# A spectral filter mixed with a state-space branch: split halves in PSUM tiles of their own, weight rows copied by ScalarE, and another written order

## The chip, the core and the metric

One core of one Trainium2 chip runs one program. The metric is device time in microseconds, the median of several executions. Engines are named as in the profile: PE (TensorE matmul) and PEld (its weight loads), DVE (VectorE), ACT (ScalarE), POOL (GpSimd) and SP (SyncE, which here issues DMAs). Each engine runs its instructions strictly in the order in which they were written; a wait at the head of a queue holds all that stands behind it.

## The reference

The input is a sequence of 2048 rows by 512 channels. Two branches are computed from it and mixed by a gate per row.

```python
x = A_x                                                   # 1 x 2048 x 512
g = sigmoid((x * gate_w).sum(-1, keepdims=True))          # one gate per row
X = rfft2(x, axes=(-2, -1)) * (w_r + 1j * w_i)            # 2048 x 257 weights
a = irfft2(X, s=(2048, 512), axes=(-2, -1))               # branch A
dt = exp(log_dt); A = -exp(log_A_real) + 1j * A_imag
K = 2 * einsum("dn,dnl->dl", C * dt, exp(A * dt * pos)).real
b = irfft(rfft(x.T, 4096) * rfft(K, 4096))[:2048].T + x * D_skip   # branch B, a causal convolution
out = g * a + (1 - g) * b
```

## The kernel before

**What is computed where.** With the given inputs `A * dt * 2048` is so small that K is constant along the sequence, and branch B is a running sum of x times one number per channel plus the skip term. The program counts on the chip for how many channels that holds (word `G4` counts, `G5` reads the count) and has a general path behind a branch, which is not taken. Branch A is a two-dimensional Fourier transform, a product with the weights, and the transform back, all in float32.

**Stages of branch A.** Each is a short function, and each has a letter; a letter with a number is a word of the written order.
- `F`, `C`, `c` (lines 254 to 284): ten parts of x (DMA into `AI`) are folded by POOL, multiplied on PE into `p_s`, and turned by DVE into `AR`. This is the first factor of the transform along the sequence.
- Then eight units, 0 to 7, each of two slots of rows. `P` (line 424) multiplies `AR` by `s2e` into `p_t`; `t` (431) copies it to `et` on ACT; `D` (440) is the transform over channels into `p_d`, with `dfw`; `d` (453) copies a part of it to `ds` on ACT; `Z` (459) forms sums and differences in `p_d` on DVE; `U` and `W` (475) are the two products with the weights `w` on DVE into `tw`. Units 3 and 5 (`ZPE`) do the sums in PE with `zfw` and skip `Z`.
- `p` (486) and `g` (494) combine the products on POOL into `px` and `gt`; `h` (506) repairs the first row on ACT; `I` (525) transforms back over channels on PE into `p_v`; `i` (533) copies a part to `po` on ACT; `V` (540) adds on DVE into `AI`.
- `K`, `B`, `b`, `Q`, `q` (548 to 603): the transform back along the sequence. `K` repairs slot 0, `B` multiplies eight blocks into `p_ia` (with `NDUM` dummy matmuls ahead of block `FIRSTB`), `b` turns them into `AR`, `Q` multiplies by `s1a` into `p_oa`, and `q` adds `XT` and stores to `out`. Every `B` needs all units; so everything from `K` on is a tail behind the last unit.

Two units, 1 and 7, are split: the words 11, 21 and 17, 27 are the halves (64 of 128 rows) of units 1 and 7. In the kernel before the two halves share one PSUM tile at each of `P`, `D` and `I`.

**Branch B and the gate.** `X` loads the transposed input into `XT`, 1 MB for each of four blocks; `x` copies to PSUM, `m` is the running sum on DVE, `o` scales by the skip factor on ACT, `y` writes the scaled sum to `v`, and `r` adds `v` to `XT` with an accumulating DMA that POOL issues. `k` multiplies `XT` by the gate weights on PE (line 376); `G1` is the sigmoid, `G2` sends the gates to DRAM, `O` loads them back spread over all partitions as `gb`, `u` copies them to PSUM, `H` multiplies `XT` by 1 - g on POOL, and `E` multiplies the constants `s1a` by g on DVE, so that `Q` gives g * a.

**Weight rows.** The weights come per unit with `l` (`w<-in_w_dram`, 512 KB). Their partition 0 needs other numbers, worked out from columns 0 and 256: `J0` does it with three DVE and two ACT instructions, `J1` turns the result with a matmul, `J2` copies it to `hT`, and `L` puts 2 KB of it into partition 0 of each unit's `w` with a DMA on SP's queue. That DMA waits until the unit's `w` has landed.

**What sets the order.** The string `PLAN` lists all words in one order, and each engine gets its share of that order. Tiles come from pools: `ps` has four PSUM tiles of two banks; `blk` has 13 SBUF tiles that `f`, `prm`, `et`, `tw`, `px`, `gt` and `gs` share; `w` and `s1a` share four; `v` and `gb` share four. A new tile waits for the last reader of the one whose place it takes. SP's queue also waits for the eighth DMA back, since eight semaphores go round.

Of the kernel before, what the change touches and what calls it, by code (L numbers as in the profile page):

```python
# [21 lines left out]
NV = 4  # L22
ZPE = (3, 5)
LASTQ = 4
FIRSTB = 1
# [22 lines left out]
def _consts():  # L48
# [91 lines left out]
    for x in range(2):  # L140
# [32 lines left out]
        "c_s2v": f32(s2v), "c_s2r": f32(s2r), "c_s2q": f32(s2q), "c_s1b": f32(s1b), "c_s1a": f32(s1a.reshape(128, 16, 2, 128).transpose(0, 2, 1, 3).reshape(128, 4, 8, 128).transpose(1, 0, 2, 3)), "c_dfw": f32(dfw), "c_zfw": f32(zfw), "c_dbw": f32(dbw),  # L173
# [5 lines left out]
def body(ctx: ExitStack, tc: tile.TileContext, x, xg, xt, w, wh, prms, vecs, gw,  # L179
         c_s1e, c_s1f, c_s2e, c_s2, c_s2v, c_s2r, c_s2q, c_s1b, c_s1a, c_dfw, c_zfw, c_dbw, c_pos, c_eye, out):  # L180
# [27 lines left out]
    last = work.tile([P, 384], F32, name="last")  # L208
    s1e, ones = last[:, 0:128], last[:, 128:256]
    hw = last[:, 256:320].rearrange("p (q r f m) -> p q r f m", q=8, r=2, f=2)  # L210
    hs = last[:, 320:352].rearrange("p (q i) -> p q i", q=8)
    few = last[:, 352:376].rearrange("p (k i) -> p k i", i=4)
    pers = work.tile([P, 16], F32, name="pers")
    s0, dsk, one, m_, nm = pers[:, 0:8], pers[:, 8:12], pers[:, 12:13], pers[:, 13:14], pers[:, 14:15]
    s2e = work.tile([P, 16, P], F32, name="s2e")
    s2v = work.tile([P, 64], F32, name="s2v")
    s2r = work.tile([P, P], F32, name="s2r")
# [3 lines left out]
    hT = work.tile([32, P], F32, name="hT")  # L221
    gws = work.tile([P, 4, 32], F32, name="gws")
# [9 lines left out]
    with tc.manual_schedule():  # L232
        prm = {}
        ldt = few[:, 0]
        nc.scalar.dma_start(s1e, c_s1e)
        nc.scalar.dma_start(hw, wh)
        nc.scalar.dma_start(eye, c_eye)
# [62 lines left out]
        def n1():  # L300
            S.activation(few[:, 0], few[:, 0], AF.Exp)
# [115 lines left out]
        def load_h(u):  # L417
            nc.sync.dma_start(t_["w", u][0:1, 0], hT[4 * u:4 * u + 4])
# [455 lines left out]
```

## Time and profile before

| | |
|---|---|
| time, median of 3 runs | 119.22 us (118.77 to 123.17) |
| the profiled execution: its own time, and its span | 119.98 us, 118.1 us |
| busy in the span | PE 96.8, PEld 78.7, DVE 88.0, ACT 45.6, POOL 75.1 us |
| mean granted PE clock | 0.969 |
| moved by DMA | 28.79 MB, mean 244 GB/s |

The span goes from the first to the last instruction; the profiled execution's own time is 1.88 us more. All rows that are quoted come from that one execution, whose own time is 0.76 us above the median. A program matmul in float32 stands as two matmuls in the trace, so the four of a half unit are eight rows. Times at the head of a row are microseconds from the start of the span. Where instructions of one engine follow each other without a wait, the time of one shown is longer than the step from one start to the next, since their ends overlap.

### The profile page before, as it was taken

The page shows a single profiled execution, that of the slowest core. Times are in us where ns is not written, and L with a number is a line of the kernel's source. Part 1 is how long each engine was busy: PE and PEld are TensorE (multiplying, and loading weights), DVE is VectorE, ACT ScalarE, POOL GpSimd, SP SyncE. Part 2 cuts the span into 40 slices and gives each one's busy share as a digit, 9 for nine tenths or more (in the row PEclk, how much of TensorE's full clock was granted, in tenths as well). Part 3 has the DMA queues.
Part 4 walks back from the last instruction along what each step waited for, and adds up shares of the span by engine and source line. Part 5 has one row for each costly group of instructions (what it writes and reads, how often), then busy time and mean ns, then how long its engine had stood idle before and what let it go on. Part 6 is the DMA issues. An engine that isn't in the chain of part 4 may idle for free.

```text
span 118.1 us, 2316 instructions
## 1 busy us (share of the span) xinstructions
PE 96.8 (82%) x877; PEld 78.7 (67%) x877; DVE 88.0 (74%) x139; ACT 45.6 (39%) x80; POOL 75.1 (64%) x70
## 2 busy tenths in 40 slices
PE   6989784999861999968495978997899999999700
PEld 6957463999430649967395977987753359999700
DVE  0059889848988439999649599999798999956620
ACT  0320004359549059391878283698740000000000
POOL 0069580220796005999999999999999999910000
PEclk9999999999999679999999999999999999999985
DMA  3999999977979976499979999978129700678680
GB/s 66 381 389 416 413 383 345 298 318 238 327 286 337 409 226 220 136 325 178 225 191 214 262 321 218 262 198 297 50 44 190 126 3 3 248 314 330 248 302 15
DMA packets 9314, 28.79 MB, mean 244 GB/s; under 512 B 1577, under 2 KB 2121, under 8 KB 8781
## 3 DMA queue, kind: packets, MB, share of 16 engines
q1 hardware_dynamic: 7628, 23.93, 55.9%
q0 software_dynamic: 1088, 4.19, 19.5%
q10 hardware_dynamic: 576, 0.43, 1.1%
q8 instruction: 9, 0.15, 0.5%
q14 instruction: 13, 0.10, 0.3%
HBM read 20.12 MB, written 4.21 MB: 206 GB/s over the span
## 4 chain that ended last, share of the span: by engine, by line
PE 46%; DMA 29%; POOL 10%; DVE 3%; ACT 3%; issue 2%; SPq 1%; DVEq 0%; POOLq 0%
PE p_oa L588 13%; PE p_d L447 10%; DMA s2e<-in_c_s2e_dram 8%; PE p_ia L565 6%; DMA XT<-in_xt_dram 6%; PE p_t L429 6%; PE p_v L531 6%; DMA AI<-in_x_dram 6%; POOL gt L504 4%; DMA s1a<-in_c_s1a_dram 4%; DMA w<-in_w_dram 3%; DMA last<-in_c_s1e_dram 3%; POOL gt L503 2%; POOL px L490 2%; PE p_gate L376 2%
## 5 line engine op out<-in xcount | busy, mean ns | idle before, releaser
L447 PE MATMUL p_d<-et,dfw 128*128 128x256 f32 (+1 forms) x80 | 18.7, 370 | 4.2 <-ACT et L434 3.2
L484 DVE TENSOR_TENSOR tw<-p_d,w 128x1024 f32<-128x1024 f32 (+1 forms) x20 | 19.2, 1005 | 1.2 <-ACT ds L456 0.6
L371 POOL TENSOR_TENSOR XT<-XT,gb 128x1024 f32<-128x1024 f32 x8 | 19.2, 2755 | 0.0
L447 PEld LDWEIGHTS p_d<-et,dfw 128*128 128x128 f32 x80 | 12.9, 202 | 8.4 <-ACT et L434 4.7
L531 PE MATMUL p_v<-dbw,gt 128*128 128x128 f32 x128 | 15.8, 278 | 2.5 <-POOL px L490 1.2
L429 PE MATMUL p_t<-s2e,AR 128*128 128x128 f32 x128 | 16.2, 282 | 1.6 <-DMA s2e<-in_c_s2e_dram 1.6
L429 PEld LDWEIGHTS p_t<-s2e,AR 128*128 128x128 f32 x128 | 15.8, 196 | 2.0 <-DVE AR L283 1.8
L531 PEld LDWEIGHTS p_v<-dbw,gt 128*128 128x128 f32 x128 | 14.9, 192 | 3.2 <-ACT gt L512 1.4
L283 DVE STREAM_TRANSPOSE AR<-p_s 128x512 f32<-128x512 f32 (+1 forms) x20 | 10.7, 587 | 7.3 <-PE p_s L275 7.3
L503 POOL TENSOR_TENSOR gt<-px 128x512 f32<-128x512 f32 (+1 forms) x10 | 11.0, 1101 | 7.8 <-PE p_d L447 7.3
L588 PEld LDWEIGHTS p_oa<-s1a,AR 128*128 128x128 f32 x128 | 15.2, 196 | 0.8 <-DVE AR L569 0.8
L588 PE MATMUL p_oa<-s1a,AR 128*128 128x128 f32 x128 | 15.3, 282 | 0.0
L490 POOL TENSOR_TENSOR px<-tw 128x512 f32<-128x512 f32 (+1 forms) x10 | 11.8, 1179 | 5.0 <-DVE tw L484 5.0
L258 POOL TENSOR_TENSOR f<-AI 128x512 f32<-128x512 f32 (+1 forms) x8 | 9.0, 1138 | 7.8 <-DMA AI<-in_x_dram 7.7
L545 DVE TENSOR_TENSOR AI<-p_v,po 128x512 f32<-128x512 f32 (+1 forms) x20 | 10.3, 574 | 2.0 <-PE p_v L531 1.3
L491 POOL TENSOR_TENSOR px<-tw 128x512 f32<-128x512 f32 (+1 forms) x10 | 11.7, 1174 | 0.0
L504 POOL TENSOR_TENSOR gt<-px 128x512 f32<-128x512 f32 (+1 forms) x10 | 11.0, 1102 | 0.0
L602 DVE TENSOR_TENSOR AI<-p_oa,XT 128x1024 f32<-128x1024 f32 x7 | 8.5, 1219 | 3.1 <-PE p_oa L588 2.6
L275 PE MATMUL p_s<-AI,last 64*64 64x128 f32 (+1 forms) x192 | 9.9, 335 | 0.5 <-DMA AI<-in_x_dram 0.5
L569 DVE STREAM_TRANSPOSE AR<-p_ia 128x1024 f32<-128x1024 f32 x8 | 9.3, 1216 | 0.5 <-PE p_ia L565 0.5
L339 DVE TENSOR_TENSOR_SCAN p_x<-p_x,XT 128x1024 f32<-128x1024 f32 x4 | 9.2, 2290 | 0.3 <-ACT p_x L336 0.3
L434 ACT COPY et<-p_t 128x1024 f32<-128x1024 f32 (+1 forms) x10 | 8.2, 845 | 2.3 <-PE p_t L429 2.2
(72 smaller groups left out, 120.2 us busy)
## 6 DMA issues: line engine op xcount, KB each, us to landing
XT<-in_xt_dram SPq DMA_DIRECT2D x4, 1024.0 KB, 7.2
w<-in_w_dram SPq DMA_DIRECT2D x8, 512.0 KB, 8.4
XT<-v POOLq DMA_DIRECT2D x4, 1024.0 KB, 9.1
out_dram<-AI SPq DMA_DIRECT2D x7, 512.0 KB, 3.4
AI<-in_x_dram SPq DMA_DIRECT2D x6, 512.0 KB, 6.2
gb<-gd SPq DMA_DIRECT2D x4, 512.0 KB, 4.0
s1a<-in_c_s1a_dram SPq DMA_DIRECT2D x4, 512.0 KB, 4.9
AI<-in_x_dram SPq DMA_DIRECT2D x4, 256.0 KB
```

The source lines that it names most:

```text
L283: V.transpose(av[:, u, :, k], pv[:, u])
L371: E.tensor_tensor(r, r, t_["gb", h % 2], op=ALU.mult)
L429: T.matmul(p[:, q, :, 64 * v:64 * v + 64], AR[:, q % 2, 8 * (q // 2) + u, :, v], s2e[:, 2 * u + v], start=True, stop=True)
L447: T.matmul(d[:, o, 1:3] if h else d[:, o, 0:4:3], dfw[:, 2 * h + o], e[:, 2 * h + o], start=True, stop=not z)
L484: E.tensor_tensor(t, z, w, op=ALU.mult)
L490: G.tensor_tensor(po[:, 0], t1[:, :, 0:4:2], t1[:, :, 1:4:2][:, :, ::-1], op=ALU.subtract)
L491: G.tensor_tensor(po[:, 1, :, ::-1], t2[:, :, 0:4:2], t2[:, :, 1:4:2][:, :, ::-1], op=ALU.add)
L503: G.tensor_tensor(gv[:, :, 0], src[0], src[1], op=ALU.subtract)
L504: G.tensor_tensor(gv[:, ::-1, 1], src[0], src[1], op=ALU.add)
L531: T.matmul(p[:, v, h, o], rows(u, o, v, h), dbw[:, h, o], start=True, stop=True)
L545: V.tensor_tensor(ai[:, :, :, k], t_["pi", u][:, v, :, 0], t_["po", u][:, v], op=ALU.subtract if k else ALU.add)
L588: T.matmul(p[:, b], VA[:, i, 8 * (k % 2) + b, :, k // 2], s1a[k][:, b], start=True, stop=True)
```

## The change

- **Halves.** `P`, `D` and `I` of a half unit each take a PSUM tile of their own (`acc`), and their columns lie together (`cut`), in `et`, `ds` and `tw` too. Which units are split is read from `PLAN`; they are still 1 and 7.
- **Weight rows.** `wh` is laid out on the host as 8 rows of 2 x 512 numbers. `J` is now two DVE instructions on 8 partitions and one DMA of ACT's queue, which puts eight rows of 512 into partition 0 of `AI` (after its x has been read). `L` is a copy on ACT from there into partition 0 of `w`. The matmul, `hs`, `hT`, the copy of it and the eight DMAs on SP's queue are gone; the identity `eye` is loaded on the path that is not taken.
- **Gated constants.** `s1a` comes as half of its columns (256 KB for each of four), since the other half differs by a sign that goes with the partition. `E` is one DVE product instead of two, and one ACT instruction that multiplies by the sign (`sgn`).
- **Small loads.** Gate weights, `log_dt`, the skip factors and the sign come in one DMA (`gv`), and `s2v` and `s2r` in one (`s2`).
- **Order.** `PLAN` is another list of the same words (without `J1` and `J2`), `FIRSTB` is 0 and `LASTQ` is 7. Unit 1 now comes ahead of unit 7.

The diff, with `PLAN` cut to its first line and what is repeated left out:

```diff
@@
+SLOT = (5, 3, 6, 7, 0, 4, 1, 2)
 ZPE = (3, 5)
-LASTQ = 4
-FIRSTB = 1
+LASTQ = 7
+FIRSTB = 0
...
-F2 X1 C0 R7 C1 c0 R6 J0 c1 F3 J1 R9 C2 c2 F4 C3 c3 F5 R1 R0 C4 J2 F6 C5 c4 C6 c5 F7 F9 T0 F8 c6 C7 c7 C8 C9 c8 c9 P17
...
+R7 R0 C1 F2 C0 c0 c1 T0 C2 c2 F3 C3 c3 F4 C4 F5 R1 C5 F6 F8 F9 c4 c5 C6 c6 C8 R9 J0 C9 c9 c8 R6 F7 C7 c7 P11 N1 l1 N0
...
+SPLIT = [int(w[2:]) for w in PLAN.split() if w[0] == "P" and w[1] == "1" and len(w) == 3]
...
-        nc.scalar.dma_start(hw, wh)
-        nc.scalar.dma_start(eye, c_eye)
+        hw = blk([P, 2, 512], "hw")[0:8]
+        nc.scalar.dma_start(hw, wh)
...
         def J_(k):
-            if k == 0:
-                V.tensor_tensor(hs[:, :, 0:4:2], hw[:, :, 0, :, 0], hw[:, :, 0, :, 1], op=ALU.add)
...
-                S.copy(hT, t_["ph"][:32, 0, 0:P])
-
+            a, b = (hw[:, z].rearrange("u (i k) -> u i k", i=4) for z in range(2))
+            V.tensor_tensor(a[:, 0:4:2], a[:, 0:4:2], b[:, 0:4:2], op=ALU.add)
+            V.tensor_tensor(a[:, 1:4:2], a[:, 1:4:2], b[:, 1:4:2], op=ALU.subtract)
+            nc.scalar.dma_start(AI[0:1, 0:8], hw[:, 0])
...
         def load_h(u):
-            nc.sync.dma_start(t_["w", u][0:1, 0], hT[4 * u:4 * u + 4])
+            S.copy(t_["w", u][0:1, 0].rearrange("p i k -> p (i k)"), AI[0:1, SLOT[u]])
...
+        def cut(t, n, v=None):
+            if len(t.shape) == 3 and t.shape[1] == 8:
+                return t
+            t = t.rearrange("p a b k -> p (a b k)" if len(t.shape) == 4 else "p a b -> p (a b)")
+            if n % 10 in SPLIT:
+                return t.rearrange("p (v g k) -> p v g k", v=2, k=64)[:, n // 10 - 1]
+            t = t.rearrange("p (g k) -> p g k", k=P)
+            return t if v is None else t[:, :, 64 * v:64 * v + 64]
+
+        def acc(name, n):
+            p = psum(name)
+            return p[:, 0].rearrange("p (g k) -> p g k", k=64) if n >= 10 else p
+
         def P_(n):
             u, r, vs = unit(n)
-            p = new(("pt", u), lambda: psum("p_t").rearrange("p k (q c r) -> p (k q) c r", q=2, c=2))
+            p = t_["pt", n] = acc("p_t", n)
...
         def D_(n):
             u, r, vs = unit(n)
-            new(("pd", u), lambda: psum("p_d"))
+            t_["pd", n] = acc("p_d", n)
...
         def I_(n):
             u, r, vs = unit(n)
-            p = new(("pi", u), lambda: psum("p_v").rearrange("p u (h o t) -> p u h o t", h=2, o=2))
+            p = t_["pi", n] = psum("p_v").rearrange("p u (h o t) -> p u h o t", h=2, o=2)
...
         def load_a(k):
-            s1a[k] = work.tile([P, 8, P], F32, tag="w", name="s1a", bufs=4)
-            nc.sync.dma_start(s1a[k], c_s1a[k])
+            s1a[k] = work.tile([P, 2, 8, 64], F32, tag="w", name="s1a", bufs=4)
+            nc.sync.dma_start(s1a[k][:, 1].rearrange("p b c -> p (b c)"), c_s1a[k])

         def gated(k, E):
-            s = s1a[k].rearrange("p b (e c) -> p b e c", e=2)
...
-            for e in range(2):
-                E.tensor_tensor(s[:, :, e], s[:, :, e], g, op=ALU.mult)
+            a = s1a[k].rearrange("p e b c -> p e (b c)")
+            g = (t_["gp", k // 2] if E is V else t_["gb", 2 + k // 2])[:, 512 * (k % 2):512 * (k % 2) + 512]
+            E.tensor_tensor(a[:, 0], a[:, 1], g, op=ALU.mult)
+            S.activation(a[:, 1], a[:, 0], AF.Copy, scale=sgn)
...
-            lambda: (nc.sync.dma_start(gws, gw), nc.sync.dma_start(dsk, vecs[:, 1])),
-            lambda: (nc.sync.dma_start(s2v, c_s2v), nc.sync.dma_start(s2r, c_s2r)),
+            lambda: nc.sync.dma_start(gv, gw),
+            lambda: nc.sync.dma_start(s2, c_s2v),
```

What the order does at three places of the program, on the engines that wait or are waited for there.

PE, from its first matmul of the unit stage (`p_t` is word `P`, `p_d` is word `D`, the number is the tile's), in the kernel before:

```order
L429 MATMUL p_t_305<-s2e_75,AR_67 128x2x64 x8
L429 MATMUL p_t_318<-s2e_75,AR_67 128x2x64 x4
L447 MATMUL p_d_328<-et_325,dfw_78 128x2x64 x8
L429 MATMUL p_t_318<-s2e_75,AR_67 128x2x64 x4
L429 MATMUL p_t_375<-s2e_75,AR_67 128x2x64 x8
L429 MATMUL p_t_385<-s2e_75,AR_67 128x2x64 x8
L447 MATMUL p_d_408<-et_367,dfw_78 128x2x64 x4
L376 MATMUL p_gate_415<-XT_72,gws_82 32x512 x4
L447 MATMUL p_d_408<-et_367,dfw_78 128x2x64 x4
L376 MATMUL p_gate_415<-XT_72,gws_82 32x512 x8
```

and in the changed kernel, where the gates `p_gate` stand 15 rows further back than this piece ends:

```order
L432 MATMUL p_t_295<-s2e_75,AR_67 128x128 x4
L432 MATMUL p_t_305<-s2e_75,AR_67 128x128 x4
L450 MATMUL p_d_319<-et_316,dfw_77 128x2x64 x2
L450 MATMUL p_d_319<-et_316,dfw_77 128x128 x2
L450 MATMUL p_d_326<-et_316,dfw_77 128x2x64 x2
L450 MATMUL p_d_326<-et_316,dfw_77 128x128 x2
L432 MATMUL p_t_340<-s2e_75,AR_67 128x128 x4
```

Before, both halves of unit 7 lie in `p_t_305` and both `D` halves of unit 1 in `p_d_408`, with gate matmuls between them; now each half has a tile, and the halves follow each other directly. Of the gate matmuls, 16 program matmuls on the four 1 MB blocks of `XT`, eight now come behind the `D` of units 1, 7, 4 and 6, and eight behind that of unit 0 too, instead of among the `D` of units 1 and 4.

POOL, from its first `px` (word `p`; `gt` is word `g`), before:

```order
L490 TENSOR_TENSOR px_432<-tw_397 128x2x2x64
L491 TENSOR_TENSOR px_432<-tw_395 128x2x2x64
L490 TENSOR_TENSOR px_432<-tw_397 128x2x2x64
L491 TENSOR_TENSOR px_432<-tw_395 128x2x2x64
L503 TENSOR_TENSOR gt_469<-px_432 128x2x2x64
L504 TENSOR_TENSOR gt_469<-px_432 128x2x2x64
L503 TENSOR_TENSOR gt_469<-px_432 128x2x2x64
L504 TENSOR_TENSOR gt_469<-px_432 128x2x2x64
L490 TENSOR_TENSOR px_478<-tw_465 128x2x2x64
```

and now:

```order
L493 TENSOR_TENSOR px_398<-tw_360 128x2x2x64
L494 TENSOR_TENSOR px_398<-tw_357 128x2x2x64
L506 TENSOR_TENSOR gt_401<-px_398 128x2x2x64
L507 TENSOR_TENSOR gt_401<-px_398 128x2x2x64
L493 TENSOR_TENSOR px_398<-tw_360 128x2x2x64
L494 TENSOR_TENSOR px_398<-tw_357 128x2x2x64
L506 TENSOR_TENSOR gt_401<-px_398 128x2x2x64
```

The first half's `gt` now stands ahead of the second half's `px`, and these are the halves of unit 1. The tile behind the third `gt` differs as well: before, `gt_553` (unit 1, two rows behind this piece) takes the place of `et_435`, which the matmuls into `p_d_458` read; now `gt_401` and `gt_457` take the places of an `f` and a `prm` tile of the first stage.

SP's DMA queue from the first weight row, before:

```order
L418 DMA w<-hT 1x4x128
L415 DMA w<-in_w_dram 128x1024 x3
L418 DMA w<-hT 1x4x128
L332 DMA XT<-in_xt_dram 128x2048
L418 DMA w<-hT 1x4x128
L332 DMA XT<-in_xt_dram 128x2048
L415 DMA w<-in_w_dram 128x1024
```

and the same stretch now, from the third weight load:

```order
L405 DMA w<-in_w_dram 128x1024
L330 DMA XT<-in_xt_dram 128x2048
L405 DMA w<-in_w_dram 128x1024
L617 DMA dbw<-in_c_dbw_dram 128x768
L330 DMA XT<-in_xt_dram 128x2048 x2
L405 DMA w<-in_w_dram 128x1024
```

The rows `L418`, each of which waits for a `w` to land, are gone from this queue; the loads of `XT` and `w` follow each other. All of `w`'s row copies now stand on ACT's queue, the first as that engine's eighth instruction behind its table load.

More of the change, by code (lines that the diff above doesn't have):

```diff
@@ L206, in body @@
     X = AF_
[L208 removed]
+    last = work.tile([P, 288], F32, name="last")
     s1e, ones = last[:, 0:128], last[:, 128:256]
[L210 to L212 removed]
+    few = last[:, 256:280].rearrange("p (k i) -> p k i", i=4)
     pers = work.tile([P, 16], F32, name="pers")
[L214 removed]
+    s0, one, m_, nm = pers[:, 0:8], pers[:, 12:13], pers[:, 13:14], pers[:, 14:15]
     s2e = work.tile([P, 16, P], F32, name="s2e")
[L216 to L217 removed]
+    s2 = work.tile([P, 192], F32, name="s2")
+    s2v, s2r = s2[:, 0:64], s2[:, 64:192]
     dfw = work.tile([P, 4, P], F32, name="dfw")
@@ L220, in body @@
     dbw = work.tile([P, 2, 3, P], F32, name="dbw")
-    hT = work.tile([32, P], F32, name="hT")
-    gws = work.tile([P, 4, 32], F32, name="gws")
+    gv = work.tile([P, 137], F32, name="gv")
+    gws, ldt, dsk = gv[:, 0:128].rearrange("p (i c) -> p i c", i=4), gv[:, 128:132], gv[:, 132:136]
+    sgn = gv[:, 136:137]
     def blk(shape, name):
@@ L530, in I_ @@
                     for o in range(2):
[L531 removed]
+                        T.matmul(p[:, v - vs[0], h, o], rows(u, o, v, h), dbw[:, h, o], start=True, stop=True)
         def i_a(n):
```

75 lines of the change are left out of this document (35 added, 40 removed).

## Prediction

> **What bounds the kernel now.** I read the stretches first: how busy each engine is, stage by stage. The columns are the stretch, its length, the busy time of PE, PEld, DVE, ACT and POOL, the granted PE clock, the DMA share and GB/s.
>
> ```profile
> core 0: us, PE busy (x) PEld busy (x) DVE busy (x) ACT busy (x) POOL busy (x), PEclk, DMA share, GB/s
> ...
> 30.00:38.00 8.00, 4.20 (x36) 2.14 (x39) 7.18 (x14) 5.13 (x8) 6.59 (x10) 1.00 0.87 308
> 38.00:42.50 4.50, 4.50 (x20) 2.50 (x24) 1.59 (x3) 0.62 (x3) 0.37 (x1) 0.63 0.97 386
> 42.50:46.00 3.50, 3.50 (x23) 2.44 (x23) 2.70 (x5) 3.43 (x5) 0.33 (x1) 0.98 0.58 162
> 46.00:60.00 14.00, 11.01 (x80) 10.25 (x79) 11.64 (x16) 8.27 (x17) 13.84 (x15) 1.00 0.85 219
> 60.00:84.00 24.00, 20.76 (x166) 19.43 (x165) 21.73 (x35) 16.47 (x31) 23.69 (x20) 1.00 0.90 241
> 84.00:89.00 5.00, 4.62 (x26) 2.90 (x27) 4.36 (x9) 2.88 (x5) 5.00 (x3) 1.00 0.27 50
> ```
>
> From 46 to 84 POOL is busy 13.84 of 14 and 23.69 of 24 us: there it sets the pace. From 38 to 46 it does 0.70 us of work in 8, and PE, busy throughout, runs at a clock of 0.63 for 4.5 us. So POOL's end is its work plus a hole, and the next question is what made the hole. The chain of waits (start us, us, what) and the waits (engine, line, what it waited for, total, times, longest) answer it.
>
> ```profile
> 23.26 1.80 PE p_d L447 x16
> ...
> 25.83 0.32 SPq L418
> 26.20 4.06 DMA w<-in_w_dram
> 30.27 0.59 SPq L418
> 30.91 7.00 DMA XT<-in_xt_dram
> 37.95 1.06 PE p_gate L376 x8
> 39.02 3.49 PE p_d L447 x8
> 42.51 1.06 PE p_gate L376 x8
> 43.57 1.92 PE p_d L447 x8
> ...
> 82.60 1.29 POOL gt L504
> 83.91 0.43 ACT gt L512
> 84.38 2.05 PE p_v L531 x16
> 86.44 0.86 PE p_k L551 x2
> 87.30 1.72 PE p_ia L559 x4
> 89.01 7.22 PE p_ia L565 x62
> 96.23 15.29 PE p_oa L588 x128
> ```
>
> ```profile
> SPq L418 <- DMA w<-in_w_dram: 12.4, 4, 5.0
> ...
> PE p_gate L376 <- DMA XT<-in_xt_dram: 3.4, 1, 3.4
> ...
> POOL gt L503 <- PE p_d L447: 7.3, 1, 7.3
> ```
>
> Read from top to bottom: SP's queue holds at the weight rows (`L418`) until `w` lands, 12.4 us in four waits; so `XT` is issued at 30.91 and lands 7.00 us later; PE, in order, stands 3.4 us at the gate matmuls, and its next eight `D` rows take 3.49 us where the eight after take 1.92; the last `D` ends at 45.49, and POOL's third `gt`, which takes the place of the `et` which that `D` reads, waits 7.3 us. The timeline of POOL (start, us, operation, and in brackets the idle time before it) has the ends of this:
>
> ```profile
> 30.26 0.73 POOL L490 TENSOR_TENSOR px<-tw 128x256 f32<-128x256 f32 x1 [3.81 <-DVE tw L484]
> ...
> 36.95 0.73 POOL L490 TENSOR_TENSOR px<-tw 128x256 f32<-128x256 f32 x1 [1.15 <-DVE tw L484]
> ...
> 45.67 0.74 POOL L503 TENSOR_TENSOR gt<-px 128x256 f32<-128x256 f32 x1 [7.30 <-PE p_d L447]
> ```
>
> So the span has four legs: up to POOL's first `px` at 30.26; from there to the end of the last `gt`, 82.60 + 1.29 = 83.89, which is 53.63 us, of them 1.15 + 7.30 = 8.45 waited and 45.18 filled; from 83.89 to the first row of `B` at 89.01, 5.12; and `B`, `Q` and the stores, 118.1 - 89.01 = 29.09.
>
> **Leg 1, to the first `px`.** Rows of the timeline where the unit stage begins:
>
> ```profile
> 15.33 3.98 DVE L283 STREAM_TRANSPOSE AR<-p_s 128x512 f32<-128x512 f32 x8 [1.09 <-PE p_s L275]
> ...
> 20.08 3.18 PE L429 MATMUL p_t<-s2e,AR 128*128 128x128 f32 x24 [1.62 <-DMA s2e<-in_c_s2e_dram]
> ```
>
> `AR` is ready at 15.33 + 3.98 = 19.31, but PE starts at 20.08, after `s2e`. That load now stands second behind x instead of fourth; the start becomes about 19.5, -0.6. Before, the copy `t` waited for both halves of a shared tile, 16 rows of 3.18 / 24 = 0.1325 us; a half in a tile of its own waits for 8, -1.06. In the same way `d` waits for 8 rows of `D` instead of 16, half of the 1.80 us at 23.26, -0.90. Together -2.6, and the first `px` comes at about 27.7. If the copies in between eat the halves' gain, -0.6 is left; -3.2 if the first `D` also no longer waits for the second half's copy, which before it did.
>
> **Leg 2, to the last `gt`.** POOL's work is the same here: ten `px`, ten `gt` and three DMA issues, 45.18 us. The hole goes only if what led to it goes: the `XT` loads no longer stand behind a wait for `w`, the gates stand behind four units' `D`, and the third `gt` takes the place of a tile of the first stage. All three are in the order of the changed kernel, so I take the 8.45 us away; the cold clock (3.49 - 1.92 = 1.57) lies inside it and isn't counted again. What is late next? Groups of one form and the DMA issues (name, KB each, median us to landing) give the prices:
>
> ```profile
> L339 DVE TENSOR_TENSOR_SCAN p_x<-p_x,XT 128x1024 f32<-128x1024 f32 x4 | 9.2, 2290 | 0.3 <-ACT p_x L336 0.3
> ...
> L343 ACT ACTIVATE XT<-XT,pers 128x1024 f32<-128x1024 f32 x8 | 9.0, 1147 | 0.0
> ...
> L582 DVE TENSOR_TENSOR s1a<-s1a,p_g 128x512 f32<-128x512 f32 x8 | 5.0, 677 | 0.0
> ...
> L537 ACT COPY po<-p_v 128x512 f32<-128x512 f32 x6 | 3.5, 575 | 2.1 <-PE p_v L531 2.1
> ...
> L511 ACT COPY gt<-px 1x256 f32<-1x256 f32 x6 | 2.6, 428 | 3.9 <-POOL gt L503 3.9
> ...
> L511 ACT COPY gt<-px 1x128 f32<-1x128 f32 x4 | 1.2, 300 | 0.0
> ...
> XT<-in_xt_dram SPq DMA_DIRECT2D x4, 1024.0 KB, 7.2
> w<-in_w_dram SPq DMA_DIRECT2D x8, 512.0 KB, 8.4
> ```
>
> - Weight rows on ACT: no 1x512 copy stands in the trace. From 300 ns for 128 and 428 for 256 elements, 128 more cost 128 ns, so 512 cost about 0.684 us; the lower bound is the 575 of the 128x512 copy. Eight are 4.6 to 5.5 us, and I take 5.5. ACT was busy 5.13 + 0.62 + 3.43 + 8.27 + 16.47 = 33.92 us from 30 to 84; with the rows 39.4, still under POOL's 45.18. So most lies beside POOL's work, but each copy stands ahead of some `et`, `ds` or `po` which PE or DVE waits for. SP loses eight issues and the 12.4 us.
> - DVE had 7.18 + 1.59 + 2.70 + 11.64 + 21.73 = 44.84 us from 30 to 84, about what POOL has. `E` falls from eight products to four, -4 x 0.677 = -2.7, of which the tail takes a part. So DVE feeds POOL with no slack to speak of.
> - The accumulating DMA `r1` now stands on POOL behind the two steps each of `px` and `gt` of unit 4, 4 x 1.29 = 5.16 us. From the same point it needs the scan (2.29) and three ACT passes (`y` and two `o`, 3 x 1.15), 5.74 us: 0.6 of wait, and 2.6 if the copy ahead of the scan is late by two `et` or row copies.
>
> Bounds for the new waits: POOL's idle share from 46 to 84, (0.16 + 0.31) / 38 = 1.2% of 45.18, so 0.6 us; and 8.45, if the hole only moves. I take 3.3: 2.6 at `r1`, and 0.7 for the thin feeding. Leg 2: -8.45 + 3.3 = -5.15; the last `gt` ends at 83.89 - 2.6 - 5.15 = 76.1.
>
> On the row copies the Trainium skill has a price: its page ScalarE: Activation LUTs (section What ACT_TABLE_LOAD costs) gives an ACTIVATE 186 ns and 0.833 ns for each element, which is 613 ns for 512, an estimate. By it eight are 4.9 us rather than 5.5; the trace's nearest rows differ both ways (575 for 128x512, 428 for 1x256), and none has that form.
>
> **Leg 3, to the first `B`.** Before: `gt`, its repair on ACT 0.43, `I` 2.05, `K` 0.86, two dummy matmuls in four rows 1.72, `B`. The dummies covered ACT's copy of `K`'s result. Now they stand behind `K1`, so that copy (0.575 for its like) is bare, and ahead of it ACT has the sign half of one `E` (0.575 to 0.72). `K0` moreover waits for `V3` on DVE, which stands behind a scan and three `V`: I take 1.0, from half of one scan (2.29 / 2 = 1.15). Sum 0.6 + 0.6 + 1.0 = +2.2, bounds 0 (all done while POOL finishes) and +4.5 (the whole scan late). `B` starts at 83.5 or so.
>
> Against moving that half of `E` speaks a rule of the same page (section Rules for kernel authors): multiplications belong on VectorE. By it the 0.6 us ahead of `K1`'s copy would be the change's own loss, and without it leg 3 were 1.6 and the time 113.1, an estimate. The trace bears that out only in part: from 84 to 89 DVE is busy 4.36 of 5 and ACT 2.88, so on DVE the 0.677 would stand in the fuller queue.
>
> **Leg 4, the tail.** `B` 7.22 and `Q` 15.29 keep their rows. Two of the four `E` (3 and 2) now lie between blocks of `B` and `Q` on DVE and ACT: 2 x (0.677 + 0.6) = 2.6 us, hidden by the first quarters of `Q`, 15.29 / 8 = 1.91 each, of which two precede `Q3`; if that cover is gone, about 1.3. POOL's eight products with 1 - g follow the last `gt` as before. I take 0.
>
> **Sum.** -2.6 - 8.45 + 3.3 + 2.2 = -5.55 against the profiled execution's own 119.98: 114.4. That execution lies 0.76 above the median of 119.22, so 113.7 for the median. 2% is about what a measurement of this kernel can tell from no change: faster is below 116.8, slower above 121.6.
>
> **Rivals.**
> - *The waits for `w` move from SP to ACT (slower).* A row copy on ACT still needs its `w`, and behind it stand `et` and `ds` for PE and DVE. If each `w` lands as late as before, ACT waits 12.4 in place of the 3.3: -2.6 - 8.45 + 12.4 + 2.2 = +3.55, and +5.1 with one more cold stretch of 1.57 us: 122.8 to 124.3. It decides from 11.3 us of such waits in all for slower by 2%, since 8.85 of gain stand against it. For it: a `w` takes 8.4 us at the median, and DMA stood at 0.87 to 0.97 of its capacity from 30 to 42.5. Against: the loads were late there since SP held them, and the first three `w` now go ahead of the first `XT` but for nothing else. The Trainium skill, TensorE: Matmul & The Clock Gate (Part 1: The HAM clock gate), has PE fall to half clock after about 3.4 us idle; the trace's wait of 3.4 us and the clock of 0.63 behind it agree.
> - *ACT becomes the bound.* All 5.5 us of row copies come on the path in place of the 3.3: -3.35, own 116.6, median 115.9; with the 3.3 as well, 119.2. For it: 39.4 us plus the sign copies, and every stage passes through ACT. Against: 54 - 39.4 still leaves it 14.6 us of idle time in that stretch.
> - *PSUM.* Twelve half tiles for `P`, `D` and `I` in place of six, from four places: six more takes, each of which may wait for one DVE product on a half, the 0.677 us of the 128x512 row. +4.1 us, median 117.8. For it: a second half's `D` now waits for a tile that a `W` of the other unit reads. Against: a half frees its tile sooner.
> - *No new wait.* Leg 2 with 0.6 and leg 3 with 0: -10.45, median 108.8; with leg 3 as forecast, 111.0.
>
> **Chances.** Forecast (111.5 to 116) 0.58; no new wait 0.12; ACT 0.14; PSUM 0.08; slower 0.08. Faster: 0.58 + 0.12 + a third of ACT's = 0.75; same: the rest of ACT's and PSUM's, 0.17; slower 0.08. The range from 109.5 to 118.0 leaves out the slower rival, part of the no-wait one and ACT's upper third, together 0.16.
>
> **What would show it.** Right: no `XT` wait at the gate matmuls and no stretch of low clock after 30; POOL's first `px` at 27 to 28.5, its third `gt` without a wait of microseconds; last `gt` at 75 to 77.5; first `B` at 82 to 85; `B` and `Q` as long as before; row copies of 0.58 to 0.7. Wrong: ACT waiting for `w` for more than 3 us; POOL idle for more than 5 us between its first `px` and last `gt`; a `Q` that waits for `s1a`.

## The result, and the profile after

The changed kernel took 113.88 us (median of four, 112.72 to 114.33) against 120.48 for the kernel before (median of four, 118.77 to 123.17): a ratio of 0.9555, with a 95% interval of 0.943 to 0.968. Ratios with an interval are of each kernel's faster executions alone (here all four now, and the 118.77 and 119.22 before); that of the two medians is 0.945. In a later comparison the same two gave 114.22 (six, 112.87 to 115.25) and 120.03, ratio 0.9607, interval 0.947 to 0.974. The forecast was 113.7. The profiled execution took 113.95 us, its span is 112.2.

The chain of waits after (start us, us, what) reaches back only to the end of POOL's last `gt`:

```profile
76.19 0.43 ACT gt L515
76.62 0.04 issue
76.66 2.07 PE p_v L534 x16
...
79.23 0.42 ACT s1a L585
...
79.86 0.58 ACT AI L556
80.44 0.04 issue
80.48 1.98 PE p_ia L562 x4
82.47 6.37 PE p_ia L568 x56
```

The engines by stretch (columns as before: PE, PEld, DVE, ACT, POOL, granted PE clock, DMA share, GB/s):

```profile
29.00:47.00 18.00, 17.07 (x129) 13.10 (x129) 15.75 (x29) 13.30 (x24) 16.20 (x20) 1.00 0.79 306
47.00:76.20 29.20, 26.84 (x208) 24.63 (x200) 28.25 (x41) 24.19 (x44) 28.77 (x24) 1.00 0.85 208
```

And POOL's rows with the idle time ahead of them, from its first `px` to its last `gt`:

```profile
29.04 0.73 POOL L493 TENSOR_TENSOR px<-tw 128x256 f32<-128x256 f32 x1 [2.20 <-DVE tw L487]
...
47.03 1.36 POOL L351 DMA_DIRECT2D XT<-v  x1 [1.40 <-ACT XT L341]
...
74.88 1.28 POOL L507 TENSOR_TENSOR gt<-px 128x512 f32<-128x512 f32 x1
```

The hole is gone: the clock stays at 1.00, the gate matmuls no longer wait for an `XT`, and POOL waits once, 1.40 us, at `r1`. But for that it is busy from its first `px` to its last `gt`, with DVE close to it (28.25 of 29.2 us). SP's queue waits little for `w` ahead of `XT`:

```profile
SPq L330 <- DMA w<-in_w_dram: 2.5, 2, 1.5
```

By the four legs of the prediction:

| leg | before | after | difference | forecast |
|---|---|---|---|---|
| 1, to the first `px` | 30.26 | 29.04 | -1.22 | -2.6 |
| 2, to the end of the last `gt` | 53.63 | 47.12 | -6.51 | -5.15 |
| 3, to the first `B` | 5.12 | 6.31 | +1.19 | +2.2 |
| 4, to the end of the span | 29.09 | 29.73 | +0.64 | 0 |
| span | 118.1 | 112.2 | -5.9 | -5.55 |

Leg 2 can be compared to a tenth of a microsecond: in five profiles of the changed kernel and of kernels that differ from it outside this leg, it is 47.11 or 47.12. Leg 1 can't: with the same code it ends between 27.35 and 29.34, as the next section shows.

### The profile page after: what moved, and what is told of

It is laid out like the page before. It is cut to its first block, busy times and chain, and to the rows that moved or that the text cites. A ratio compares the mean times of both kernels' runs of the same rounds, so it can differ in the third digit from the quotient of the medians.

```text
span 112.2 us, 2292 instructions
## 1 busy us (share of the span) xinstructions
PE 96.8 (86%) x876; PEld 78.1 (70%) x876; DVE 85.9 (77%) x134; ACT 51.5 (46%) x89; POOL 75.5 (67%) x70
## 5 line engine op out<-in xcount | busy, mean ns | idle before, releaser
L432 PE MATMUL p_t<-s2e,AR 128*128 128x128 f32 x128 | 17.0, 286 | 2.9 <-DVE AR L283 1.6
L450 PE MATMUL p_d<-et,dfw 128*128 128x256 f32 (+1 forms) x80 | 16.8, 343 | 0.8 <-ACT v L346 0.3
L534 PE MATMUL p_v<-dbw,gt 128*128 128x128 f32 x128 | 15.2, 276 | 1.6 <-ACT gt L515 1.6
L450 PEld LDWEIGHTS p_d<-et,dfw 128*128 128x128 f32 x80 | 12.0, 191 | 3.5 <-ACT gt L515 1.1
L275 PE MATMUL p_s<-AI,last 64*64 64x128 f32 (+1 forms) x192 | 10.7, 362 | 0.7 <-DMA AI<-in_x_dram 0.7
L506 POOL TENSOR_TENSOR gt<-px 128x512 f32<-128x512 f32 (+1 forms) x10 | 10.6, 1061 | 0.8
L507 POOL TENSOR_TENSOR gt<-px 128x512 f32<-128x512 f32 (+1 forms) x10 | 10.6, 1059 | 0.0
```

The lines of the kernel that those rows point to most:

```text
L275: T.matmul(p[64 * g:64 * g + 64, h, u * n:u * n + n], s1e[r, 64 * u * i:64 * u * i + 64], src[:, g * n:g * n + n], start=i == 0, stop=i == ...
L432: T.matmul(cut(p, n, v)[:, 2 * q:2 * q + 2], AR[:, q % 2, 8 * (q // 2) + u, :, v], s2e[:, 2 * u + v], start=True, stop=True)
L450: T.matmul(d[:, o, 1:3] if h else d[:, o, 0:4:3], dfw[:, 2 * h + o], e[:, 2 * h + o], start=True, stop=not z)
L506: G.tensor_tensor(gv[:, :, 0], src[0], src[1], op=ALU.subtract)
L507: G.tensor_tensor(gv[:, ::-1, 1], src[0], src[1], op=ALU.add)
L534: T.matmul(p[:, v - vs[0], h, o], rows(u, o, v, h), dbw[:, h, o], start=True, stop=True)
```

## The experiments

### Is it the gates behind a late XT that made the hole?

The kernel before, with the gate matmuls (`k`) moved behind `D6`, and SP's queue as it was:

```diff
-D11 d11 k0 D21 k1 k2 p17 t6 D4 X3 y0 Z11 d21 l5 k3 R10 D6 U11
+D11 d11 D21 p17 t6 D4 X3 y0 Z11 d21 l5 R10 D6 k0 k1 k2 k3 U11
```

> The kernel before with one thing moved: the four groups of gate matmuls stand behind the D of unit 6, where before they stood among the halves of D of unit 1 and ahead of that of units 4 and 6. Nothing else differs; the weight rows still go by SP's queue, which still waits 12 us for w. Theory 1 (the hole of POOL came from a D that stood behind gate matmuls, and these behind an XT that SP's waits had made late): POOL's third gt waits less than 1.5 us instead of 7.3, and the time falls by 4 to 7 us, to 112 to 116 against 119.2. Theory 2 (the hole would come in any case, since XT is as late as before and everything behind the gates on PE waits for it): PE's wait at the gates stays at 3 us or more, POOL waits somewhere else, and less than 2 us are gained.

117.59 us (four, 115.42 to 117.86) against 120.45 (seven, 118.46 to 122.67): 2.9 us less (3.0 between the fastest of each), with no overlap of the two sets. POOL's rows:

```profile
32.13 0.73 POOL L490 TENSOR_TENSOR px<-tw 128x256 f32<-128x256 f32 x1 [3.80 <-DVE tw L484]
...
38.63 0.74 POOL L490 TENSOR_TENSOR px<-tw 128x256 f32<-128x256 f32 x1 [0.96 <-DVE tw L484]
...
47.46 1.26 POOL L490 TENSOR_TENSOR px<-tw 128x512 f32<-128x512 f32 x1 [1.71 <-DVE tw L484]
...
51.75 1.29 POOL L503 TENSOR_TENSOR gt<-px 128x512 f32<-128x512 f32 x1 [1.78 <-ACT gt L512]
```

The third `gt` waits no more: the 7.30 us are gone with nothing changed but the place of the gates. So the gates ahead of that `D` are shown to be what held POOL; that their `XT` came late because SP waited for `w` is not tried by this run, which left those waits as they were. Not all of it is won: two new waits, 1.71 and 1.78, come in its place, and leg 2 falls from 53.6 to 49.6, by 4.0. Theory 1 had the mechanism and, in leg 2, the size; the whole time fell by less than its 4 to 7, because leg 1 was 1.9 us longer in the profiled execution, in which the first 24 rows of `P` took 4.59 us at a clock of 0.69 instead of 3.18 at 1.00.

### The rows on SP again, in the new order

```diff
-            S.copy(t_["w", u][0:1, 0].rearrange("p i k -> p (i k)"), AI[0:1, SLOT[u]])
+            nc.sync.dma_start(t_["w", u][0:1, 0].rearrange("p i k -> p (i k)"), AI[0:1, SLOT[u]])
```

> The changed kernel with one thing undone: each weight row again goes by a DMA on SP's queue (2 KB, from the same row that ScalarE would copy from), at the same places of the written order. ScalarE has eight copies less. Theory 1 (the order alone would remove most of the hole, since the gates stand behind the D of four units; the rows on ScalarE add little): 0 to +2 us, 113.9 to 116; SP waits for w again for some us, XT comes later, but PE's wait at the gates stays under 1.5 us. Theory 2 (it is SP's freed queue that gains): +4 to +7 us, with PE waiting at the gates and POOL with a hole again. Theory 3 (ScalarE's copies are on the path): faster by 1 us or more.

127.61 us (127.02 to 127.88), 7.1% slower than the kernel before (interval 6.1 to 8.1%). It is 13.7 us above the 113.88 of the changed kernel: the direction of theory 2, at twice its size; theory 1, that the order alone would do, falls. Waits of SP, of DVE and of POOL:

```profile
SPq L408 <- DMA w<-in_w_dram: 15.9, 5, 6.0
...
SPq L408 <- DMA AI<-hw: 6.9, 1, 6.9
```

```profile
DVE tw L487 <- DMA w<-AI: 12.1, 4, 9.5
```

```profile
POOL px L493 <- DVE tw L487: 10.3, 2, 8.2
...
POOL XT L351 <- ACT XT L341: 6.1, 2, 4.2
```

SP waits again, also for J's own DMA, which comes late in the new order; and DVE waits up to 9.5 us for a 2 KB row. To see whether J's lateness was the cause, the same was run with all of `J` moved ahead:

```diff
-F4 C4 F5 R1 C5
+F4 C4 J0 F5 R1 C5
...
-C8 R9 J0 C9
+C8 R9 C9
```

> The weight rows by SP's queue again, in the changed kernel's order, but with all of J (its two DVE instructions and its DMA) ahead, behind the matmuls of the fifth part of x. In the first such kernel SP waited 6.9 us for J's DMA at the first row, 15.9 us for w, and DVE 12.1 us for rows. Theory A (most of its +13 us came from J's late DMA, which held all of SP's loads): SP's wait for J is gone, and the time is 114 to 119. Theory B (it is SP's waits for w, and rows that land late behind other transfers, whatever J does): SP still waits 12 us or more for w, DVE still waits for rows, and the time is 121 to 128.

126.21 us (124.25 to 126.75). The wait for J is gone, and SP waits longer for `w` instead:

```profile
SPq L408 <- DMA w<-in_w_dram: 25.5, 5, 6.7
```

Theory B holds: in this order a queue that waits for `w` costs some 12 us, whatever J does. PE waited 4.5 us at the gates again, although they stand behind the `D` of four units.

### The old order in the new code

The plan of the kernel before, without `J1` and `J2`, `J0` in the place of `J2`, and its `FIRSTB` and `LASTQ`:

```diff
-LASTQ = 7
-FIRSTB = 0
+LASTQ = 4
+FIRSTB = 1
...
-R7 R0 C1 F2 C0 c0 c1 T0 C2 c2 F3 C3 c3 F4 C4 F5 R1 C5 F6 F8 F9 c4 c5 C6 c6 C8 R9 J0 C9 c9 c8 R6 F7 C7 c7 P11 N1 l1 N0
+F2 X1 C0 R7 C1 c0 R6 c1 F3 R9 C2 c2 F4 C3 c3 F5 R1 R0 C4 J0 F6 C5 c4 C6 c5 F7 F9 T0 F8 c6 C7 c7 C8 C9 c8 c9 P17
...
```

> The new code in the old order: tiles for halves, rows copied by ScalarE, half of the gated constants, but the words stand as in the kernel before (J0 at the place where the last part of J was, FIRSTB 1 and LASTQ 4). Theory 1 (SP no longer waits, so XT is issued some 5 to 9 us earlier and the gates among the D halves find it there; the hole shrinks from 7.3 to under 3 us): 114 to 117. Theory 2 (only the order helps; ScalarE now waits for w in SP's place, ahead of the t and d copies): 118 to 123, with waits of ScalarE for w of 3 us or more.

122.16 us (118.81 to 124.55), which can't be told from the 118.46 to 122.67 of the kernel before. SP no longer waits for `w`, the gate matmuls wait for no `XT`, and POOL's longest hole in the place of the 7.3 is 1.58 us, as theory 1 had it, which bears out the part of the chain that starts at SP; but ScalarE now pays. Its rows near the end:

```profile
64.51 1.14 ACT L408 COPY w<-AI 1x512 f32<-1x512 f32 x2 [3.96 <-DMA w<-in_w_dram]
...
75.28 1.11 ACT L346 ACTIVATE v<-p_x,pers 128x1024 f32<-128x1024 f32 x1 [3.96 <-DVE p_x L337]
...
81.93 0.57 ACT L540 COPY po<-p_v 128x512 f32<-128x512 f32 x1
82.40 0.42 ACT L514 COPY gt<-px 1x256 f32<-1x256 f32 x1
```

It waits 3.96 us for a `w`, as theory 2 had it (the second 3.96, at 75.28, is a wait for DVE's scan), and the chain of waits lies on ScalarE's queue alone from 78.77 to 83.14, where two passes for `XT`, two `po` and a sign half of `E` stand ahead of a `gt` for which PE waits 2.84 us. That the wait for `w` is what made this queue late is argued, not shown. Leg 2 is 51.8 us, with a hole of 3.11 for DVE near its end; leg 3 is 7.3 instead of 5.1, and leg 4 is 2.0 longer, nearly all of it behind PE's last row. So neither the new rows in the old order nor the new order with the old rows gains; the gain needs both.

### The halves in one tile again

With the old, alternating columns (`shared`, which also takes them back in `cut`), and with the new ones, each half in a bank of its own (`shared_cols`). Both have this edit:

```diff
         def acc(name, n):
-            p = psum(name)
-            return p[:, 0].rearrange("p (g k) -> p g k", k=64) if n >= 10 else p
+            return new((name, n % 10), lambda: psum(name))
...
-            p = t_["pi", n] = psum("p_v").rearrange("p u (h o t) -> p u h o t", h=2, o=2)
+            p = t_["pi", n] = new(("pi", u, 0), lambda: psum("p_v").rearrange("p u (h o t) -> p u h o t", h=2, o=2))
```

> The changed kernel with the halves undone: the two halves of units 1 and 7 again share one PSUM tile at each of P, D and I, and their columns alternate as before; order, rows and constants stay. From my working: t and d of the first half wait for 8 more matmul rows each (1.06 and 0.90), so POOL's first px comes about 2.0 us later, at 31.0 instead of 29.0, and the time is 115.0 to 116.5 if nothing behind absorbs it. Rival: the shared tiles also tie the halves of D together later on (the first half's Z and W wait for the second half's D), and it is 3 us or more. Second rival: the order has enough slack, and it is under 1 us.

> The changed kernel with the two halves of a split unit in one PSUM tile again at P, D and I, but with the new columns (each half lies together, in a bank of its own). Theory 1 (what counts is the tile: a tile shared by two halves makes the first half's t and d wait for the second half's matmuls, or comes free only when both are read): 119 to 123, as with the old columns. Theory 2 (what counts is that the halves' columns lie apart, so that reads of one half need not wait for the other): within 1 us of the changed kernel.

123.03 us (122.52 to 124.22) and 123.42 (121.91 to 125.12): 9 us above the changed kernel, and the columns make no difference. What counts is the tile. From the first `P` to the first sum on DVE it is 6.41 us in both, against 3.85 in the changed kernel (two rows of ScalarE and one of DVE in `shared`, then DVE's row in the changed kernel):

```profile
24.78 0.37 ACT L458 COPY ds<-p_d 128x256 f32<-128x256 f32 x1 [0.76 <-PE p_d L449]
...
26.40 0.37 ACT L458 COPY ds<-p_d 128x256 f32<-128x256 f32 x1 [1.25 <-PE p_d L449]
...
26.80 0.36 DVE L466 SCALAR_TENSOR_TENSOR p_d<-p_d,pers,ds 128x128 f32<-128x128 f32 x1 [4.11 <-ACT ds L458]
```

```profile
24.94 0.36 DVE L467 SCALAR_TENSOR_TENSOR p_d<-p_d,pers,ds 128x128 f32<-128x128 f32 x1 [1.55 <-ACT ds L459]
```

That is 2.6 us at the start, where the working had 1.96 (1.06 at `t` and 0.90 at `d`), and it lies partly elsewhere. `t` starts 2.55 us behind the first `P` instead of 1.61, near the 1.06; the first `d` comes 1.84 us behind `t` in both kernels, so the 0.90 isn't there; and the first sum comes 2.02 us behind the first `d` instead of 0.40, since with a shared tile it waits until the second half's `D` and `d` are done too. The order also leans on these tiles later: leg 2 is 51.6 and 50.9 us instead of 47.1, with 5.1 to 5.7 us of POOL's waits, and leg 3 is 7.9. The first rival had this: 3 us or more, because the halves are tied together further on.

### Single prices in the changed kernel

**Row copies left out** (`load_h` does nothing, so that partition 0 of each `w` keeps what the load put there).

> The changed kernel without the eight copies of weight rows on ScalarE (partition 0 of each w keeps what the load put there, so the first row of each unit is worked out with other weights; everything else is computed). It prices those copies in place: 8 x 0.61 = 4.9 us of ScalarE. Theory (they lie beside POOL's work; the bare places are one wait of DVE and one of PE for such a copy, 0.5 us each): 0 to 1.2 us faster. Rival (ScalarE is the bound and every copy is on the path): 3 to 5 us faster.

112.84 us (six, 112.31 to 114.25), 1.0 to 1.4 under the changed kernel's two medians. Leg 2 falls from 47.12 to 46.30 us, the wait at `r1` from 1.40 to 0.53:

```profile
46.80 1.36 POOL L351 DMA_DIRECT2D XT<-v  x1 [0.53 <-ACT XT L341]
```

So 4.8 us of copies cost 0.8 of leg 2, all of it in the wait at `r1`; the rest lie beside POOL's work. The theory holds.

**The sign half of `E` on DVE.**

```diff
-            S.activation(a[:, 1], a[:, 0], AF.Copy, scale=sgn)
+            E.tensor_scalar(a[:, 1], a[:, 0], sgn, None, op0=ALU.mult)
```

> The changed kernel with the sign half of the four E worked by DVE (one instruction with a number per partition) instead of ScalarE, 0.72 us each there. From the trace, E0's sign stands ahead of the copy of K's result on ScalarE, which the dummies and the first B wait for. Theory (that 0.5 us is on the path, DVE has 0.4 us idle at that place): the first B 0.2 to 0.5 us earlier, time 0.1 to 0.6 us lower. Rival (DVE delays the last V by as much as is won, and the two E between the turns of B delay Q): 0 to +1 us.

118.12 us (six, 114.79 to 120.6), against 113.88 and 114.22 for the changed kernel. The profiled execution is one of the two at 114.8; what the four from 117.12 up lost, no trace shows. In the profile legs 3 and 4 take 38.4 us (112.9 - 74.47) instead of 36.0 (112.2 - 76.16): 2.4 us slower, more than the rival had. The first `B` comes 0.2 us earlier after the last `gt`, but then `Q` waits (PE):

```profile
93.43 2.12 PE L591 MATMUL p_oa<-s1a,AR 128*128 128x128 f32 x16 [1.41 <-DVE s1a L584]
96.40 9.69 PE L591 MATMUL p_oa<-s1a,AR 128*128 128x128 f32 x80 [0.85 <-DVE AR L572]
```

since DVE needs up to 2.09 us for the product (its rows):

```profile
81.22 0.72 DVE L585 TENSOR_SCALAR s1a<-s1a,gv 128x512 f32<-128x512 f32 x1
...
90.60 2.09 DVE L585 TENSOR_SCALAR s1a<-s1a,gv 128x512 f32<-128x512 f32 x1
```

The rule that the prediction weighed (the Trainium skill, ScalarE: Activation LUTs, Rules for kernel authors: multiplications on VectorE) would have made the kernel slower here. The price that the same page of the Trainium skill gives for an ACTIVATE (section What ACT_TABLE_LOAD costs), by which a row copy would take 613 ns, an estimate, was right: the eight took 611 ns each.

```profile
L408 ACT COPY w<-AI 1x512 f32<-1x512 f32 x8 | 4.8, 611 | 0.0
L585 ACT ACTIVATE s1a<-s1a,gv 128x512 f32<-128x512 f32 x4 | 2.8, 731 | 0.8 <-DVE s1a L584 0.8
```

**J's two DVE instructions first of all**, to explain why the first `P` started at 21.09 and not at 19.5.

```diff
-R7 R0 C1 F2 C0
+J0 R7 R0 C1 F2 C0
...
-C8 R9 J0 C9
+C8 R9 J1 C9
...
+            if k == 0:
                 V.tensor_tensor(a[:, 0:4:2], a[:, 0:4:2], b[:, 0:4:2], op=ALU.add)
                 V.tensor_tensor(a[:, 1:4:2], a[:, 1:4:2], b[:, 1:4:2], op=ALU.subtract)
+            else:
                 nc.scalar.dma_start(AI[0:1, 0:8], hw[:, 0])
```

> The changed kernel with the two DVE instructions of J at the head of DVE's order, ahead of all turns (their input lands with the first parts of x), and only J's DMA left at the old place. Theory (the first P started at 21.1 and not at the 19.5 of my working, since J's two instructions, 0.37 and 1.48 us, stood ahead of the last three pairs of turns): the last turn ends about 1.0 us earlier, POOL's first px comes at 28.0 to 28.4 and the time falls by 0.5 to 1.2 us from 113.9. Rival (PE's own rows for the last parts of x end at 19.5, and the turns follow them in any case; the late start comes from the load of x): less than 0.3 us.

112.78 us (six, 111.68 to 113.41), first `px` at 27.50. This looks like the theory, but kernels with `J` in its old place have 27.35 and 27.72 too. DVE's rows of `J` in the changed kernel and here:

```profile
17.61 1.48 DVE L400 TENSOR_TENSOR hw<-hw 8x256 f32<-8x256 f32 x1
19.02 2.62 DVE L283 STREAM_TRANSPOSE AR<-p_s 128x256 f32<-128x256 f32 x6
```

```profile
4.66 0.41 DVE L401 TENSOR_TENSOR hw<-hw 8x256 f32<-8x256 f32 x1
```

From the end of PE's last rows for x to the end of the last turn it took 2.11 us in the changed kernel's profile, 1.39 here, and 1.38 in the kernel with the sign on DVE, where `J` stood in its old place but its second instruction took 0.94. So J's place costs between nothing and 0.7 us, by the execution; the rest of the lateness is the load of x (PE's last rows for it end at 19.53 there, at 18.46 in the kernel before, and between 18.27 and 19.48 in other profiles with the same code up to there). Theory and rival each have a part.

**The changed kernel once more.**

> The changed kernel once more, unchanged, beside the next one. POOL's first px came at 29.0 in its first profile and at 27.4 and 27.7 in two kernels that share its code up to there, after loads of x that ended at other times. Theory (leg 1 varies with the load of x, and the working's 27.7 is as good as the 29.0): first px between 27.2 and 29.2, the stretch from first px to last gt again 47.1, time 112.5 to 114.5.

Its first `px` came at 29.34, a little past the 29.2; leg 2 is 47.11; 114.22 us. The start shows a second thing that varies (PE's first rows of `P` here, then in the first profile of the same kernel):

```profile
19.83 3.28 PE L432 MATMUL p_t<-s2e,AR 128*128 128x128 f32 x16 [1.56 <-DVE AR L283]
```

```profile
21.09 2.52 PE L432 MATMUL p_t<-s2e,AR 128*128 128x128 f32 x16 [1.56 <-DVE AR L283]
```

Here `P` starts 1.26 us earlier, but its rows take 3.28 us instead of 2.52, since the granted clock (the third column from the end of that stretch's row) was 0.69; the gain is lost by the first `px`.

```profile
19.80:25.30 5.50, 5.37 (x30) 5.18 (x31) 2.36 (x5) 2.50 (x5) 0.64 (x3) 0.69 1.04 410
```

**Without the dummy matmuls** (`NDUM = 0`).

> The changed kernel without the two dummy matmuls ahead of the first B. In its trace they start at 80.48, behind ScalarE's copy of K's result, and take 1.98 us, and the last V ends at 80.66. Theory (they no longer cover anything and stand bare on the path): the first B starts at about 80.8 instead of 82.4, and the time falls by 1.4 to 1.9 us. Rival (they keep PE's clock up for B and Q, so that without them a stretch of lower clock costs as much): a granted clock under 0.9 in the first us of B, and less than 0.7 us gained.

112.20 us (six, 111.44 to 113.47), 1.7 to 2.0 under the changed kernel's two medians, which come from other comparisons. Leg 3 falls from 6.24 to 4.32 us by the start of `B`'s rows; `B` keeps its pace (6.43 us for 56 rows, as before):

```profile
79.16 6.43 PE L568 MATMUL p_ia<-AI,s 64*64 64x512 f32 x56 [0.90 <-ACT AI L556]
```

The theory holds: behind ScalarE's copy the dummies covered nothing, and the clock in `B` is 1.00 without them. Of the 1.92 us this execution kept 1.18, since it ended 7.5 us behind PE's last row instead of 6.8.

**Without the dummies, and `r1` behind the `px` of unit 6.**

```diff
-NDUM = 2
+NDUM = 0
...
-G2 r1 p6 O0
+G2 p6 r1 O0
```

> The changed kernel without the two dummy matmuls, and with the accumulating DMA r1 one step further back on POOL, behind the px of unit 6 instead of ahead of it. Theory (r1's wait of 1.40 us for ScalarE is partly covered, since the px of unit 6 can start at about 46.6, when its first product is there, and not at 45.6): the stretch from first px to last gt falls from 47.1 to 46.1 to 46.7; the one from last gt to the first B from 6.2 to 4.3 as without the dummies; together 2.3 to 2.9 us less than the kernel of the same call. Rival (the px only waits for DVE in place of ScalarE): 1.9 us less, all of it the dummies'.

113.81 us (six, 113.31 to 115.17): no better than the changed kernel. The `px` waits longer than `r1` did, and later PE runs slower (POOL's row, then PE's last `I`, then two stretches by engine):

```profile
46.56 1.27 POOL L493 TENSOR_TENSOR px<-tw 128x512 f32<-128x512 f32 x1 [2.21 <-ACT gt L515]
```

```profile
76.02 3.19 PE L534 MATMUL p_v<-dbw,gt 128*128 128x128 f32 x16 [2.22 <-ACT gt L515]
```

```profile
72.50:76.00 3.50, 1.30 (x12) 1.10 (x10) 2.86 (x5) 1.17 (x4) 3.42 (x4) 1.00 1.03 225
76.00:79.50 3.50, 3.48 (x17) 3.33 (x18) 1.88 (x3) 1.59 (x3) 3.50 (x2) 0.60 0.98 206
```

The last `I` took 3.19 us at a clock of 0.60, where it took 2.07 in the changed kernel. Its wait for ScalarE was 1.59 us with `r1` unmoved; that moving `r1` made it 2.22 is likely, but not shown. So leg 3 is 5.73 us instead of 4.32.

Leg 2 is 47.8 us, 0.6 more than with `r1` unmoved: the rival had the cause (the `px` only waits for something else) but not that it costs. The kernel without dummies and with `r1` in its place has the lowest median of this study, 112.20, though the 112.78 of the one with J ahead can't be told from it.

## Why the prediction was right, point by point

- **What bounded the kernel.** The chain from SP's wait for `w` over `XT`, the gates and the `D` to POOL's `gt` was right: moving the gates alone removed the 7.30 us, and where SP didn't wait for `w`, in the old order with the new code, the gates didn't wait for `XT`. That the order of the changed kernel takes the hole away was right for its time, but "all three are in the order" was too much: with the rows back on SP's queue the same order has holes of 8.2 and 4.2 us. The rows on ScalarE are a condition, as the slower rival's own argument (the loads were late since SP held them) had it.
- **Leg 1, -2.6.** The term of the halves came out as a sum: from first `P` to first sum 3.85 us instead of 5.78, -1.93 against -1.96. Its parts did not: `t` started 0.55 us earlier behind `P` and not 1.06, the first `d` 1.00 earlier behind `t` and not 0.90, and 0.38 came from the first sum, which before waited for the second half's `d` too. The working had no such wait; that the total fits is in part luck. The term of the start, -0.6, failed in the profiled execution (+1.0: `P` at 21.09); in others with the same code up to there it was at 19.40 and 19.78. It was mis-sized by treating the load of x as fixed, and by leaving J's two instructions out. The leg's range (-0.6 to -3.2) held what the leg came to: 27.35 to 29.34, so -0.9 to -2.9; but the two profiles of the changed kernel itself, at 29.04 and 29.34, lie behind the 27 to 28.5 that it gave as a sign of being right.
- **Leg 2, -8.45 + 3.3.** The new wait stood where the working put it, at `r1` behind ScalarE's passes, with 1.40 us instead of 2.6. The 0.7 for thin feeding doesn't show, for POOL has no other wait; its work filled 0.55 us more (47.12 - 1.40 = 45.72 against 45.18). Most of that is the new order of POOL's own rows: more `gt` stand directly behind the `px` that they read, and of the half units such a `gt` starts 0.80 to 0.82 us behind its `px`, where other steps take 0.69. Taking 3.3 between bounds of 0.6 and 8.45 was 1.35 too much.
- **Leg 3, +2.2.** The two causes on ScalarE were there: 0.42 of `E`'s sign and 0.58 of the copy ahead of bare dummies. The wait of `K0` for `V3`, 1.0, was not: `K0` followed the last `I` directly. Measured +1.19.
- **Leg 4, 0.** +0.64, of which the stretch from the first `B` to the end of `Q` has 0.47 (105.45 - 82.47 = 22.98 against 111.52 - 89.01 = 22.51); that the two `E` between them are covered held only with the sign on ScalarE.
- **The errors cancelled.** Leg 1 gave 1.4 less, leg 2 1.4 more, leg 3 cost 1.0 less and leg 4 0.6 more. The sum was 0.35 off, by luck: the single terms were not as good as that.
- **The rivals.** Waits for `w` on ScalarE decided nothing in the changed kernel, but the same code in the old order shows them (3.96 us at once): that each `L` stands late enough behind its load is, as I read it, what keeps them away. ScalarE as the bound: its copies cost 0.8 of their 4.8. PSUM: the waits of PE's weight loads for DVE that could be of this kind are 0.8 and 0.4 us, POOL shows no wait behind them, and undoing the halves is what brought waits.

## What to carry to other kernels

A hole on the busiest engine is best traced back through the queues to the first wait that others inherit; one move at that place showed the cause, but what it gained was half of the hole, since new waits came up behind it. An order that is planned for certain buffers and queues is part of them: here each of the three that were undone alone, the rows, the halves and the order, cost 8 to 14 us, though the whole was worth 6. The halved constants and the merged small loads were not undone by themselves. Filler work that covers a wait has to be looked at again when the wait it covers has moved.

## What the hardware showed that I had not expected

- The same DVE product of 128x512 with a number per partition took 0.72 us at 81.22, where POOL went from its products to a DMA issue (at 81.59), and 1.87 to 2.09 us in the three cases beside POOL's products. J's second instruction likewise took 1.48 us where POOL was folding x, and 0.41 at the head of the program, where POOL was idle. The Trainium skill, SBUF — State Buffer (section Who interferes with whom), has DVE and GpSimd share a pair of ports, which a DVE instruction with two SBUF inputs, or one like this product, may have to wait for; both observations agree with it, though no run here tried the cause by itself.
- PE's clock fell after shorter waits than the 3.4 us of the kernel before: to 0.60 behind one of 2.22 us, when PE had been busy only 1.30 of the 3.5 us ahead; and to 0.69 behind one of 1.56 us at the first `P` in one execution of the changed kernel, but not in the other. The kernel before kept 1.00 at its first `P` behind 1.62 us; with the gates moved, but the same code up to there, it fell to 0.69 behind 1.61. So a wait of 3.4 us is not needed in these runs, and the length of the wait alone doesn't decide.
- A row of 2 KB took 9.00 us to land in the middle of the program; the median of the eight was 5.9 (chain of waits of the kernel with the rows on SP):

```profile
63.57 9.00 DMA w<-AI
```
